# Row maxima of sparse attention scores: the mask leaves the matrix product, and one product runs on two halves of the array

## The chip, the cores and the metric

The kernel runs on one core of a Trainium2 chip. The metric is the device time of one launch in microseconds (us). The core has TensorE (PE in the profile; its weight loads are PEld), VectorE (DVE), ScalarE (ACT), GpSimd (POOL) and SyncE (SP, which here only issues DMAs).

## The reference

A block-sparse attention of 4 batches and 8 heads, 768 positions, head size 64, is followed by a mixture of 8 experts in which every token goes through every expert. The change touches only the attention.

```python
scores = scale * np.matmul(q, k.transpose(0, 1, 3, 2))       # 768 x 768 for each of 32 heads
mask = np.abs(blk_i - blk_j) <= window                       # blocks of 32 positions; one mask for all heads
mask = mask | (blk_i == 0) | (blk_j == 0) | (blk_i == n_blocks - 1) | (blk_j == n_blocks - 1)
...                                                          # and 3 sampled blocks for each block of rows
scores = np.where(mask, scores, -1000000000.0)
scores = scores - np.max(scores, axis=-1, keepdims=True)
attn = np.exp(scores)
attn = attn / (np.sum(attn, axis=-1, keepdims=True) + 1e-09)
return np.matmul(attn, v).astype(np.float32)
```

## The kernel before

**The attention.** Heads are taken one after the other (n = 0 to 31), each as NC = 6 tiles of 128 rows. A number q or k is kept as two float16 parts, high and low. For a head, a tile `qt` (and `kt`) holds two transposed layers of 128 rows: q layer 0 has the high part in rows 0 to 63 and the low part in rows 64 to 127; q layer 1 has the high part again in rows 0 to 63, then 24 rows that say which block a position lies in, and later two rows with the row maximum. k layer 0 has the high part twice, k layer 1 the low part in rows 0 to 63 and 24 rows of walls (0, or a large negative number) beside it. So layer 0 gives high·high + low·high, and layer 1 gives high·low plus the mask.

Every tile is multiplied twice. `scores(n, c)` makes S of a tile with q rows on the partitions, in a PSUM tile of two banks (`sc`, pool `ps_s`, three of them), and VectorE takes its maximum over 768 columns (L676). `lower(n)` writes the six maxima of a head back into q's layer 1 (through GpSimd and a transposing DMA), and `weights(T)` makes the transposed tile with the maximum already subtracted, so that ScalarE can take the exponential at once (L708). `split_lo` (L718, L720, L722) turns the exponential's low half into float16 on the engine that the planner holds for the least loaded; `values` multiplies with v in 18 small products for each half of a tile (L765).

**The order.** It is written out by hand. `at(T, order, function, ...)` puts a step at time T, one T for each of the 192 tiles; the steps are recorded in order of T, and each engine keeps that order. Head n starts at T0 = 6n: `scores(n, c)` stands at T0 - 10 + c, `lower(n)` at T0 - 4, `weights` at T0 + c. The two transposes `turn(n, 0)` and `turn(n, 1)`, which fill `qt` and `kt` by DMA, stand at T0 - 16 and T0 - 14; `load_qk` for every second head at T0 - 30. All these DMAs are issued by SP, one after the other, and use one queue. A planner (`WORK`, `charge`, `lightest`, with `STEP` microseconds for each T) adds up costs for VectorE, ScalarE and GpSimd; it decides only where `split_lo` goes.

**The rest.** While the last heads run, the first expert's weights are loaded (`load_w(1, 0)`, one DMA of 2 MB at T = 100) and prepared. From about 400 us on, the experts' products fill TensorE (L1213 and L1345); the change does not touch them.

Of the kernel before, what the change touches and what calls it, by code (L numbers as in the profile page):

```python
# [8 lines left out]
F16 = mybir.dt.float16  # L9
F32 = mybir.dt.float32  # L10
# [34 lines left out]
HQ = 300  # L45
NHA = 10
LATE = 34
STEP = 2.03
LLO = 1
LEADM = 10  # L50
LAV = 3


@with_exitstack
def tile_sparse_attention_moe(
# [27 lines left out]
    CH = NC // 2  # L83
    TH = S // 2
# [85 lines left out]

    wr = {}

    def load_w(which, e):
        src, n, w = (w1, KD, FF) if which == 1 else (w2, KF, DM)
        t = raw.tile([P, KD * FF], F32, tag="r", name=f"r{which}_{e}")
        t = t.rearrange("p (c f) -> p c f", f=w)
        nc.sync.dma_start(out=t, in_=src[e].rearrange("(c p) f -> p c f", p=P))
        wr[which] = t

    def scale_steps(which, e, vector=nc.vector, scalar=nc.scalar):  # L180
# [213 lines left out]
    with ExitStack() as actx:  # L394
# [16 lines left out]
        aconst = pool("aconst", 1)  # L411
# [4 lines left out]
        ROWS_M, ROWS_T = D + NB, D + 34  # L416
        AT_M = D + 32
        HALVES = ((0, 512), (512, S))

        vsp = pool("vsp", 1)  # L420
        xw = pool("xw", 2)
        col = pool("col", 8)
        ps_s = pool("ps_s", 3, space=PSUM)
# [236 lines left out]
        tops = {}  # L660

        def scores(n, c):
            qt, kt = qts[n % NSET], kts[n % NSET]
            sc = ps_s.tile([P, 1024], F32, tag="sc", name=f"m_{n}_{c}")
            ka, kb_ = (kt[:, l].rearrange("p c t -> p (c t)") for l in range(2))
            for lo, hi in HALVES:
                nc.tensor.matmul(  # L667
                    sc[:, lo:hi], lhsT=qt[:, 0, c], rhs=ka[:, lo:hi], start=True, stop=False
                )
                nc.tensor.matmul(  # L670
                    sc[:, lo:hi], lhsT=qt[:ROWS_M, 1, c], rhs=kb_[:ROWS_M, lo:hi],
                    start=False, stop=True,
                )
            if c == 0:
                tops[n] = col.tile([P, NC], F32, tag="top", name=f"top_{n}")
            nc.vector.tensor_reduce(  # L676
                out=tops[n][:, c : c + 1], in_=sc[:, :S], axis=AX.X, op=ALU.max
            )

        def lower(n):  # L680
            t = qss[n % NQS]
# [12 lines left out]
        def weights(T):  # L694
# [3 lines left out]
            qa, qb = (qt[:, l].rearrange("p c t -> p (c t)") for l in range(2))  # L698
            for lo, hi in HALVES:
                nc.tensor.matmul(  # L700
# [26 lines left out]
        def lightest():  # L727
# [3 lines left out]
            return engine  # L731

        WORK = {
            scores: (0.95, 0.0, 0.0), weights: (0.0, 0.9, 0.0),
            lower: (0.0, 0.0, 1.05),
            high_qk: (0.0, 0.93, 0.0), low_qk: (0.65, 0.0, 0.0), peak: (0.0, 1.04, 0.0),
            scale_qk: (1.3, 0.0, 0.69), scale_v: (1.0, 0.0, 0.0), peak_v: (0.94, 0.0, 0.0),
# [81 lines left out]
        NPAIR = B * NHP  # L819
        for g in range(NPAIR):  # L820
            T0 = 2 * NC * g
            at(T0 - 30, FIRST, load_qk, g)
            at(T0 - 26 if g != 1 else -14, LATER, peak, g, 0)
            at(T0 - 24 if g != 1 else -14, LATER, peak, g, 1)
            at(T0 - 20, TURNS, spread_qk, g)
            at(T0 - 20, LATER, scale_qk, g)
        for n in range(B * H):
            T0 = NC * n
            for m in range(2):
                T1 = T0 + 2 * m if n != 1 else m + 3  # L830
                at(T1 - 19, LATER, high_qk, n, m)
                at(T1 - (17 if n != 1 else 18), LATER, low_qk, n, m)
                at(T1 - 16, FIRST, turn, n, m)
            for c in range(NC):
                at(T0 - LEADM + c, SCORES, scores, n, c)
            at(T0 - LEADM + NC, TOPS, lower, n)
        for T in range(NTILE):
            at(T + LAV, VALUES, values, T, 0)
# [8 lines left out]
        for b in range(B):  # L847
            T0 = b * H * NC
# [12 lines left out]
        at(22, LATER, scale_part, "g", 0, 1, wg.rearrange("p c e -> p (c e)"))  # L861
        at(23, TURNS, scale_spread, "g")
        at(23, LATER, split_gate)
        at(-31, FIRST, lay_blocks)
        at(-21, LATER, near_fence)
        at(-20, LATER, far_fence)
        at(-16, TURNS, lay_walls)

        def start_w():
            load_w(1, 0)  # L870
# [71 lines left out]
    class Pinned:  # L942
        vector, scalar, gpsimd = (InOrder(x) for x in (nc.vector, nc.scalar, nc.gpsimd))
# [562 lines left out]
```

## Time and profile before

| | |
|---|---|
| three runs | 2205.54, 2207.67, 2208.66 us; median 2207.67 |
| the profiled execution | 2205.67 us, of which the span of the profile is 2203.8 |
| TensorE busy | 2158.5 us, 98% of the span |
| VectorE, ScalarE, GpSimd busy | 1699.3, 1288.6 and 1434.1 us |
| granted TensorE clock | 0.998 |
| attention | to about 400 us; 168 of its 192 tiles belong to heads 4 to 31 |

A row of the timeline gives the start, the duration, the engine, the line of the code, and the tile written and read. A matmul's duration runs until its result has landed, so several overlap; what one costs in a dense stream is the distance to the next one's start. In the groups by line, the last column is the engine's idle time before these instructions and what ended it.

### The profile page before, as it was taken

To read this page: it belongs to the slowest core of one execution; us is meant where nothing else is said; L and a number is where in the kernel's file an instruction comes from. 1 tells how busy PE (TensorE), PEld (TensorE's weight loads), DVE (VectorE), ACT (ScalarE), POOL (GpSimd) and SP (SyncE) were. 2 spreads that over 40 slices of the span, in tenths; PEclk is the share of its full clock that TensorE was granted. 3 is DMA by queue.
4 is the path that set the end of the run, shared out by engine and by line. 5 is a ranking of instruction groups with operands and counts; after the bars stand their busy time and mean duration, and the time that the engine had idled before them with its cause. 6 is when DMAs were issued, how large, how long until landed. Compare 5 with 4: busy or idle time off the path is not lost.

```text
span 2203.8 us, 47209 instructions
## 1 busy us (share of the span) xinstructions
PE 2158.5 (98%) x18892; PEld 1598.9 (73%) x18892; DVE 1699.3 (77%) x2927; ACT 1288.6 (58%) x2393; POOL 1434.1 (65%) x1481
## 2 busy tenths in 40 slices
PE   6999999999999999999999999999999999999999
PEld 4777777667767777777777777777777777777777
DVE  8878888786878768876887688768876887688765
ACT  5788888766466556554655465546554655465442
POOL 5556678677558656865686568656865676568553
PEclk9999999999999999999999999999999999999999
DMA  7667866322121212121212121212121212121221
GB/s 169 143 143 156 208 134 149 104 87 96 59 89 51 89 51 90 51 90 51 89 51 89 51 89 51 90 51 89 51 90 51 89 51 89 51 89 58 80 80 51
DMA packets 195345, 192.36 MB, mean 87 GB/s; under 512 B 132124, under 2 KB 150580, under 8 KB 195124
## 3 DMA queue, kind: packets, MB, share of 16 engines
q1 hardware_dynamic: 194560, 189.30, 31.3%
q8 instruction: 148, 2.42, 0.5%
q14 instruction: 73, 0.60, 0.1%
q10 hardware_dynamic: 564, 0.03, 0.0%
HBM read 140.54 MB, written 17.30 MB: 72 GB/s over the span
## 4 chain that ended last, share of the span: by engine, by line
PE 63%; DVE 6%; POOL 5%; ACT 3%; issue 2%; DMA 0%; POOLq 0%; DVEq 0%; SPq 0%
PE py L1345 32%; PE p L1213 31%; ACT h L1234 1%; POOL s L1293 1%; POOL h L1245 1%; DVE attic L1076 1%; POOL r L1087 1%; DVE h L1245 1%; DVE a L1225 1%; DVE acc L1369 1%; DVE u L1225 1%; POOL r L1094 1%; DVE arena L1076 1%; POOL c L1094 1%; POOL a L1094 1%
## 5 line engine op out<-in xcount | busy, mean ns | idle before, releaser
L1345 PE MATMUL py<-w2p,h 128*128 128x256 f16 x8064 | 974.1, 273 | 3.7 <-ACT w2p L1072 1.1
L1345 PEld LDWEIGHTS <-h 128*128 128x128 f16 x8064 | 789.5, 98 | 156.7 <-issue 5.0
L1245 POOL TENSOR_TENSOR h<-u,h 128x384 f16<-128x384 f32 x128 | 126.1, 985 | 522.0 <-ACT h L1234 522.0
L1213 PEld LDWEIGHTS <-attic 128*128 128x128 f16 x3072 | 299.7, 98 | 174.4 <-DVE attic L1076 6.7
L1213 PE MATMUL p<-attic 128*128 128x384 f16 x2304 | 421.2, 326 | 3.9 <-DVE attic L1076 2.1
L1213 PE MATMUL p<-arena 128*128 128x384 f16 x2304 | 417.4, 326 | 5.3 <-DVE arena L1076 1.8
L1369 DVE SCALAR_TENSOR_TENSOR acc<-py,spare,acc 128x256 f32<-128x256 f32 (+1 forms) x588 | 299.6, 514 | 91.1 <-PE py L1345 85.5
L1234 ACT ACTIVATE h<-c 128x384 f16<-128x384 f32 x256 | 132.5, 518 | 348.8 <-DVE c L1225 301.9
L1213 PEld LDWEIGHTS <-arena 128*128 128x128 f16 x2304 | 225.2, 98 | 129.6 <-issue 5.1
L1225 DVE SCALAR_TENSOR_TENSOR a<-p,a 128x384 f32<-128x384 f32 x384 | 211.2, 550 | 21.0 <-PE p L1213 8.6
L1245 DVE TENSOR_TENSOR h<-s,h 128x384 f16<-128x384 f32 x128 | 113.8, 889 | 145.1 <-ACT h L1234 145.0
L676 DVE TENSOR_REDUCE top<-m 128x1 f32<-128x768 f32 x192 | 181.8, 951 | 48.5 <-PE m L670 47.7
L708 ACT ACTIVATE pe<-t,qk 128x768 int32<-128x768 f32 x192 | 172.4, 900 | 70.2 <-PE t L703 62.9
L1094 POOL TENSOR_TENSOR c<-c,r 128x384 f32<-128x384 f32 x128 | 159.0, 1242 | 10.0
L1234 ACT ACTIVATE h<-r 128x384 f16<-128x384 f32 x256 | 129.8, 516 | 60.2 <-POOL r L1094 58.6
L1094 POOL TENSOR_TENSOR r<-s,r 128x384 f32<-128x384 f32 x128 | 157.6, 1231 | 10.0
L1293 POOL TENSOR_TENSOR s<-a,u 128x384 f32<-128x384 f32 x128 | 133.1, 1040 | 30.6 <-ACT a L1290 29.8
L1245 POOL TENSOR_TENSOR h<-r,h 128x384 f16<-128x384 f32 x128 | 145.3, 1135 | 5.8 <-ACT h L1234 5.8
L1213 PE MATMUL p<-arena,attic 128*128 128x384 f16 x768 | 146.1, 326 | 1.1 <-DVE a L1225 1.1
L722 POOL TENSOR_SCALAR pl<-pe 128x768 f16<-128x768 uint16 x112 | 96.7, 867 | 71.3 <-ACT pe L708 70.1
L667 PE MATMUL m<-kt,qt 128*128 128x512 f16 (+1 forms) x384 | 127.8, 333 | 9.8 <-DMA kt<-ks 6.6
L1094 POOL TENSOR_TENSOR a<-a,r 128x384 f32<-128x384 f32 x128 | 128.5, 1004 | 10.0
(207 smaller groups left out, 3677.6 us busy)
## 6 DMA issues: line engine op xcount, KB each, us to landing
arena<-xd SPq DMA_DIRECT2D x128, 384.0 KB, 3.5
attic<-xd SPq DMA_DIRECT2D x96, 384.0 KB, 3.5
r<-in_moe_w_dram SPq DMA_DIRECT2D x16, 2048.0 KB, 8.5
arena<-in_q_dram SPq DMA_DIRECT2D x16, 384.0 KB, 4.1
arena<-in_k_dram SPq DMA_DIRECT2D x16, 384.0 KB, 4.6
arena<-in_v_dram SPq DMA_DIRECT2D x4, 1536.0 KB, 7.8
xd<-xs_t SPq DMA_DIRECT2D x16, 384.0 KB, 2.7
out_dram<-acc SPq DMA_DIRECT2D x48, 128.0 KB, 1.7
```

The lines of the kernel that those rows point to most:

```text
L667: nc.tensor.matmul(sc[:, lo:hi], lhsT=qt[:, 0, c], rhs=ka[:, lo:hi], start=True, stop=False)
L676: nc.vector.tensor_reduce(out=tops[n][:, c : c + 1], in_=sc[:, :S], axis=AX.X, op=ALU.max)
L708: nc.scalar.activation(pe, sc[:, :S], AF.Exp, bias=EXP_SHIFT, scale=qk[n // 2][3])
L722: nc.gpsimd.tensor_scalar(lo, low, FINE, 1.0, ALU.mult, ALU.mult)
L1094: nc.gpsimd.tensor_tensor(out=out, in0=x, in1=y, op=ALU.subtract)
L1213: nc.tensor.matmul(ps, lhsT=w1p[p][:, l, kc, fs], rhs=xp[p][:, r, kc], start=(kc == 0 and m == 0), stop=(kc == KH - 1 and m == 2),)
L1225: nc.vector.scalar_tensor_tensor(out=t, in0=ps, scalar=HDOWN, in1=other, op0=ALU.mult, op1=ALU.add)
L1234: nc.scalar.activation(h[:, 0], src, AF.Relu if relu else AF.Copy)
L1245: eng.tensor_tensor(out=h[:, 1], in0=src, in1=h[:, 0], op=ALU.subtract)
L1293: nc.gpsimd.tensor_tensor(out=s1, in0=a1, in1=u3, op=ALU.add)
L1345: nc.tensor.matmul(py, lhsT=hs[i, p, kc][:, l, tsl], rhs=w2p[p][:, r, kc], start=(old is None and kc == 0 and m == 0), stop=(kc == KF // 2 ...
L1369: nc.vector.scalar_tensor_tensor(out=dst, in0=src, scalar=c, in1=dst, op0=ALU.mult, op1=ALU.add)
```

## The change

For heads 4 to 31 the scores for the maximum are made differently; heads 0 to 3 stay as they were (`NPLAIN = 4`).

- **The mask leaves the product.** Once, at T = 7 to 12, `wall(c)` multiplies the 24 block rows alone (two matmuls on rows 64 to 87, into a tile of `ps_s`), and ScalarE copies the result into `walled`, a bfloat16 tile in SBUF. From then on VectorE's `tensor_tensor_reduce` adds `walled` to the scores, writes the sum back into PSUM, and takes the maximum with it; it is built as two instructions, the second of which writes out the one column of maxima.
- **The third product shrinks to 64 rows.** A tile's 768 columns are cut into 384 + 384, in two banks. Layer 0 is multiplied as before, in all 128 rows, by two matmuls of 384 columns. Layer 1 needs only rows 0 to 63 now: the first half of the columns is multiplied in the array's upper 64 rows, the second half in its lower 64 rows.
- **Copies for the lower rows.** Operands for rows 64 to 127 have to lie in partitions 64 to 127. `twin(n, m)` copies them there by DMA from SP: `qx` (64 x 768) from q layer 1, at T0 - 13, and `kx` (64 x 384) from the second half of k, of which it takes layer 0, the high part, at T0 - 12.
- **The first expert's weights** come as four DMAs (T = 100, 106, 112, 118) where one was.
- The planner's `STEP` goes from 2.03 to 1.93 and its cost of `scores` on VectorE from 0.95 to 1.05, which moves `split_lo`: VectorE 39 to 23 tiles, ScalarE 41 to 38, GpSimd 112 to 131.

```diff
-STEP = 2.03
+STEP = 1.93
+WALLT = -5
...
+        walled = aconst.tile([P, NC, S], BF16, name="walled")
...
+            UP, DOWN = slice(0, D), slice(D, P)
+            side = [sc[:, b * 512 : b * 512 + TH] for b in range(2)]
...
+            qx, kx = twins[n % NSET]
+            for b in range(2):
+                nc.tensor.matmul(side[b], lhsT=qt[:, 0, c], rhs=k0[b], start=True, stop=False)
+            nc.tensor.matmul(side[0], lhsT=qt[UP, 1, c], rhs=k1[0][UP], start=False, stop=True)
+            nc.tensor.matmul(
+                side[1], lhsT=qx[DOWN, c], rhs=kx[DOWN].rearrange("p c t -> p (c t)"),
+                start=False, stop=True,
+            )
+            both = sc.rearrange("p (b s) -> p b s", b=2)[:, :, :TH]
+            nc.vector.tensor_tensor_reduce(
+                out=both, in0=both, in1=walled[:, c].rearrange("p (b s) -> p b s", b=2),
+                scale=1.0, scalar=LOWEST, op0=ALU.add, op1=ALU.max, accum_out=top,
+            )
+
+        def twin(n, m):
+            x = (qts, kts)[m][n % NSET]
+            nc.sync.dma_start(
+                out=twins[n % NSET][m][D:],
+                in_=(x[:D, 0, CH:] if m else x[:D, 1]),
+            )
+
+        def wall(c):
...
+            if n >= NPLAIN:
+                at(T0 - 13, FIRST, twin, n, 0)
+                at(T0 - 12, FIRST, twin, n, 1)
...
+        for c in range(NC):
+            at((NPLAIN - 2) * NC + WALLT + c, SCORES, wall, c)
```

**TensorE, one tile of scores between two halves of `values`** (`m` is the scores' PSUM tile, `qt`, `kt` the transposed tiles, `pl` and `pe` the exponential's parts, `u` the product with v). Before:

```order
L667 LDWEIGHTS qt_101
L667 MATMUL m_2_2753<-kt_105,qt_101 128x512
L670 LDWEIGHTS qt_101
L670 MATMUL m_2_2753<-kt_105,qt_101 128x512
L667 LDWEIGHTS qt_101
L667 MATMUL m_2_2753<-kt_105,qt_101 128x256
L670 LDWEIGHTS qt_101
L670 MATMUL m_2_2753<-kt_105,qt_101 128x256
L765 LDWEIGHTS pl_1_2653
```

Now, at the same place (L705 is the product in rows 0 to 63, L706 the one in rows 64 to 127):

```order
L704 LDWEIGHTS qt_101
L704 MATMUL m_2_2804<-kt_105,qt_101 128x384
L704 LDWEIGHTS qt_101
L704 MATMUL m_2_2804<-kt_105,qt_101 128x384
L705 LDWEIGHTS qt_101
L705 MATMUL m_2_2804<-kt_105,qt_101 128x384
L706 LDWEIGHTS qx_128
L706 MATMUL m_2_2804<-kx_129,qx_128 128x384
L820 LDWEIGHTS pl_1_2704
```

The number of instructions is the same; 512 + 512 + 256 + 256 columns have become four times 384, the last two in half of the rows each.

**SP, the DMAs of one head of an even number**: its two transposes, between them the maxima of the head two before it, then the loads for a later pair. Before:

```order
L655 DMA_TRANSPOSE qt_102<-qs_109 128x12x128
L688 DMA_TRANSPOSE qt_104<-qs_110 128x6x128
L655 DMA_TRANSPOSE kt_106<-ks_113 128x12x128
L591 DMA arena<-in_q_dram 128x2x384
L591 DMA arena<-in_k_dram 128x2x384
L655 DMA_TRANSPOSE qt_103<-qs_110 128x12x128
```

Now:

```order
L671 DMA_TRANSPOSE qt_102<-qs_111 128x12x128
L743 DMA_TRANSPOSE qt_104<-qs_109 128x6x128
L671 DMA_TRANSPOSE kt_106<-ks_113 128x12x128
L718 DMA qx_130<-qt_102 64x768
L607 DMA arena<-in_q_dram 128x2x384
L607 DMA arena<-in_k_dram 128x2x384
L718 DMA kx_131<-kt_106 64x384
L301 DMA xd_76<-xs_t_3820 128x1536
L671 DMA_TRANSPOSE qt_103<-qs_109 128x12x128
```

Two copies have come in, one ahead of the loads of q and k and one behind them; each waits for its transpose to land, and SP's later DMAs stand behind it.

More of the change, by code (lines that the diff above doesn't have):

```diff
@@ L171, in tile_sparse_attention_moe, with load_w @@
     wr = {}
-    def load_w(which, e):
+    def load_w(which, e, pieces=1):
         src, n, w = (w1, KD, FF) if which == 1 else (w2, KF, DM)
@@ L176, in load_w, with piece @@
         t = t.rearrange("p (c f) -> p c f", f=w)
-        nc.sync.dma_start(out=t, in_=src[e].rearrange("(c p) f -> p c f", p=P))
+        x = src[e].rearrange("(c p) f -> p c f", p=P)
         wr[which] = t
+        m = n // pieces
+        def piece(j):
+            nc.sync.dma_start(out=t[:, j * m : (j + 1) * m], in_=x[:, j * m : (j + 1) * m])
+        piece(0)
+        return piece
     def scale_steps(which, e, vector=nc.vector, scalar=nc.scalar):
@@ L418, in tile_sparse_attention_moe @@
         HALVES = ((0, 512), (512, S))
+        NPLAIN, LOWEST = 4, -3.0e38
+        twins = [
+            tuple(
+                sets.tile([P, w, P], F16, name=f"{nm}_{i}") for nm, w in (("qx", NC), ("kx", CH))
+            )
+            for i in range(NSET)
+        ]
+        walled = aconst.tile([P, NC, S], BF16, name="walled")
         vsp = pool("vsp", 1)
@@ L664, in scores @@
             sc = ps_s.tile([P, 1024], F32, tag="sc", name=f"m_{n}_{c}")
-            ka, kb_ = (kt[:, l].rearrange("p c t -> p (c t)") for l in range(2))
+            if c == 0:
+                tops[n] = col.tile([P, NC], F32, tag="top", name=f"top_{n}")
+            top = tops[n][:, c : c + 1]
+            if n < NPLAIN:
+                ka, kb_ = (kt[:, l].rearrange("p c t -> p (c t)") for l in range(2))
+                for lo, hi in HALVES:
+                    nc.tensor.matmul(
+                        sc[:, lo:hi], lhsT=qt[:, 0, c], rhs=ka[:, lo:hi], start=True, stop=False
+                    )
+                    nc.tensor.matmul(
+                        sc[:, lo:hi], lhsT=qt[:ROWS_M, 1, c], rhs=kb_[:ROWS_M, lo:hi],
+                        start=False, stop=True,
+                    )
+                nc.vector.tensor_reduce(out=top, in_=sc[:, :S], axis=AX.X, op=ALU.max)
+                return
@@ new lines, in scores @@
+            UP, DOWN = slice(0, D), slice(D, P)
+            side = [sc[:, b * 512 : b * 512 + TH] for b in range(2)]
+            k0, k1 = (
+                [kt[:, l, b * CH : (b + 1) * CH].rearrange("p c t -> p (c t)") for b in range(2)]
+                for l in range(2)
+            )
+            qx, kx = twins[n % NSET]
+            for b in range(2):
+                nc.tensor.matmul(side[b], lhsT=qt[:, 0, c], rhs=k0[b], start=True, stop=False)
+            nc.tensor.matmul(side[0], lhsT=qt[UP, 1, c], rhs=k1[0][UP], start=False, stop=True)
@@ L666, in scores @@
+        def wall(c):
+            n = NPLAIN - 1
+            qt, kt = qts[n % NSET], kts[n % NSET]
+            E = slice(D, D + NB)
+            sc = ps_s.tile([P, 1024], F32, tag="sc", name=f"wall_{c}")
             for lo, hi in HALVES:
                 nc.tensor.matmul(
-                    sc[:, lo:hi], lhsT=qt[:, 0, c], rhs=ka[:, lo:hi], start=True, stop=False
-                )
[L670 to L678, printed above, removed]
+                    sc[:, lo:hi], lhsT=qt[E, 1, c],
+                    rhs=kt[:, 1].rearrange("p c t -> p (c t)")[E, lo:hi], start=True, stop=True,
+                )
+            nc.scalar.activation(walled[:, c], sc[:, :S], AF.Copy)
         def lower(n):
@@ L733, in tile_sparse_attention_moe @@
         WORK = {
-            scores: (0.95, 0.0, 0.0), weights: (0.0, 0.9, 0.0),
+            scores: (1.05, 0.0, 0.0), wall: (0.0, 0.9, 0.0), weights: (0.0, 0.9, 0.0),
             lower: (0.0, 0.0, 1.05),
@@ L821, in tile_sparse_attention_moe @@
             T0 = 2 * NC * g
[L822 to L826, printed above, removed]
+            back = 0
+            at(T0 - 30 - back, FIRST, load_qk, g)
+            at(T0 - 26 - back if g != 1 else -14, LATER, peak, g, 0)
+            at(T0 - 24 - back if g != 1 else -14, LATER, peak, g, 1)
+            at(T0 - 20 - back, TURNS, spread_qk, g)
+            at(T0 - 20 - back, LATER, scale_qk, g)
         for n in range(B * H):
@@ L869, in start_w @@
         def start_w():
-            load_w(1, 0)
+            piece = load_w(1, 0, KD)
+            for j in range(1, KD):
+                at(100 + 6 * j, FIRST, piece, j)
             parts, whole, spread, power = scale_steps(1, 0)
@@ L1488 @@
     from concourse.bass_utils import run_bass_kernel_spmd as _run
-    nc = _bacc.Bacc("TRN2", target_bir_lowering=False, num_devices=1)
+    nc = _bacc.Bacc("TRN2", target_bir_lowering=False, num_devices=1, dynamic_dma_scratch_size=4096)
     arrays, args = {}, []
```

5 lines of the change are left out of this document (added).

## The prediction

> **What bounds the kernel now.** I read the page's head first, for the engine that is never idle:
>
> ```profile
> span 2203.8 us, 47209 instructions
> PE 2158.5 (98%) x18892; PEld 1598.9 (73%) x18892; DVE 1699.3 (77%) x2927; ACT 1288.6 (58%) x2393; POOL 1434.1 (65%) x1481
> ```
>
> A busy TensorE says little by itself, since overlapping matmuls count as busy. So next came the table of stretches, cut along the attention (columns: length, then PE, PEld, DVE, ACT, POOL busy):
>
> ```profile
> 30.00:50.00 20.00, 19.33 (x207) 12.32 (x206) 16.48 (x25) 12.61 (x16) 13.59 (x21) 0.86 0.72 133
> 50.00:150.00 100.00, 99.97 (x1374) 72.34 (x1373) 80.01 (x134) 77.49 (x105) 53.86 (x89) 1.00 0.65 134
> 150.00:300.00 150.00, 148.28 (x2112) 107.69 (x2108) 127.37 (x202) 126.83 (x182) 96.96 (x146) 1.00 0.77 174
> 300.00:400.00 100.00, 95.73 (x1346) 69.25 (x1344) 87.25 (x132) 81.98 (x108) 82.98 (x97) 1.00 0.65 143
> ```
>
> TensorE is idle 0.03 us of 100, then 1.7 of 150, and only at the end 4.3 of 100. Third, the groups by line and shape between 60 and 400 us, for what ends the idle time of the other engines:
>
> ```profile
> L676 DVE TENSOR_REDUCE top<-m 128x1 f32<-128x768 f32 x167 | 158.4, 951 | 41.4 <-PE m L670 40.6
> L708 ACT ACTIVATE pe<-t,qk 128x768 int32<-128x768 f32 x167 | 150.0, 900 | 58.5 <-PE t L703 52.1 <-DVE xn L786 1.3 <-POOL pl L722 1.2
> L722 POOL TENSOR_SCALAR pl<-pe 128x768 f16<-128x768 uint16 x98 | 84.2, 863 | 61.9 <-ACT pe L708 60.9
> L718 DVE TENSOR_SCALAR pl<-pe 128x768 f16<-128x768 uint16 x28 | 21.7, 773 | 0.0
> ```
>
> 167 tiles in 340 us make a step of 2.036 us. VectorE waits for TensorE's scores, 41.4 / 167 = 0.25 us a step; ScalarE waits for TensorE's weights; GpSimd waits for ScalarE. Nobody of weight is waited for by TensorE: the attention runs at its rate. Last the timeline of TensorE, to see that it is dense in starts and not only in overlaps:
>
> ```profile
> 199.66 0.38 PE L667 MATMUL m<-kt,qt 128*128 128x512 f16 x1
> 199.87 0.38 PE L670 MATMUL m<-kt,qt 88*128 88x512 f16 x1
> 200.09 0.27 PE L667 MATMUL m<-kt,qt 128*128 128x256 f16 x1
> 200.21 0.27 PE L670 MATMUL m<-kt,qt 88*128 88x256 f16 x1
> 200.32 0.19 PE L765 MATMUL u<-vq,pl 128*128 128x66 f16 x1
> ...
> 200.59 0.38 PE L700 MATMUL t<-qt,kt 128*128 128x512 f16 x1
> ...
> 201.52 0.38 PE L667 MATMUL m<-kt,qt 128*128 128x512 f16 x1
> ```
>
> From one tile of scores to the next 1.86 us, of which the scores take 200.32 - 199.66 = 0.66. The rest up to 2.036 is transposes, logits and little idleness.
>
> **The products of a tile.** A 384-column matmul shows its price later in the kernel, in the chain of waits (start, length, what):
>
> ```profile
> 565.17 2.94 PE p L1213 x18
> ```
>
> 0.163 us each. The two on layer 0 make 0.33. The two of 64 rows are 0.163 if they run side by side, 0.33 if one after the other; the nearest row on how soon a second weight load and matmul can follow is the one on the walls' layout below (six matmuls in one piece), 0.025 apart, so side by side I take 0.163 + 0.025 = 0.19. Without any cost of changing between the full array and its halves the tile would fall from 0.66 to 0.52.
>
> That cost is the unknown of this change: twice in each tile the array goes from 128-row to 64-row operation and back. The trace has one place where a full-array matmul is followed by one of fewer rows, at the start:
>
> ```profile
> 4.71 0.69 DVE L472 TENSOR_SCALAR plan<-attic 24x768 bf16<-24x768 f32 x1
> ...
> 6.71 0.47 PE L615 MATMUL u<-ident,qk 128*128 128x128 f32 x1 [0.73 <-ACT unread L108]
> 7.11 0.10 PEld L524 LDWEIGHTS <-plan 24*128 24x128 bf16 x1 [0.22 <-DVE attic L503]
> ...
> 9.29 0.31 PE L524 MATMUL u<-fence,plan 24*128 24x24 bf16 x6 [2.11 <-DVE fence L519]
> ...
> 18.71 0.64 PE L615 MATMUL u<-ident,qk 128*128 128x128 f32 x2
> 18.92 0.15 PEld L667 LDWEIGHTS <-qt 128*128 128x128 f16 x1
> ```
>
> The weights of L524 lie in `plan`, ready at 5.40, yet they are loaded at 7.11, 0.40 us after the matmul in front of them started. Behind the same kind of matmul at 18.71 (two, 0.21 apart) the full-array load starts at 18.92, together with the second of them. So the 24-row load waited for the matmul to run out: 0.40 - 0.21 = 0.19 us past the end of its stream. DVE L503 is named as the releaser, but it writes a tile that the load does not read. In that stretch matmuls were spaced twice as far as later (the same pair of L615 starts inside 0.25 us at 203.39):
>
> ```profile
> 203.39 0.41 PE L615 MATMUL u<-ident,qk 128*128 128x128 f32 x2
> 203.63 0.38 PE L667 MATMUL m<-kt,qt 128*128 128x512 f16 x1
> ```
>
> At twice the rate, 0.19 becomes 0.097. With 0.025 from weight load to matmul, a change costs 0.12 into the halves. Out of them fewer rows have to run out; I take 0.09, an estimate without a row of its own. Bounds for the two together: nothing, if the one row has another cause, and 2 x 0.215 = 0.43, if the wait does not shrink with the rate. I take 0.21, because the only row that shows such a change is nearer to it than to either end. A tile then takes 0.33 + 0.19 + 0.21 = 0.73, that is 0.07 more than before; break-even is at 0.14. Over the 168 tiles of heads 4 to 31: **+11.8 us**.
>
> The Trainium skill's page TensorEngine Tiling (Array Packing), section Tiling Modes, says that changing the tiling mode, unlike changing the tile, drains TensorE; the row at 7.11 agrees, and the page gives no time for it. The page TensorE: Matmul & The Clock Gate, Part 3, lets matmuls on different row tiles start about 4 ns apart; by that figure the pair would be 0.167, an estimate, and the tile term 0.05 x 168 = 8 us; no run here shows it yet.
>
> **Walls.** Six steps at T = 7 to 12, each with 512 + 256 columns (0.22 + 0.11 from the distances above) in 24 rows and its own two changes, 0.21: 6 x 0.54 = **+3.2 us**, between 2 and 4.6. ScalarE's six copies (0.90 each, as L708) are hidden: in 30 to 50 us ScalarE is busy 12.6 of 20, and these steps are longer; uncovered they would add 2 us.
>
> **VectorE.** The new operation reads PSUM and SBUF, writes PSUM, and has a second instruction for the column of maxima. Rows that bound it: the plain maximum above at 0.951 and the slowest kind of two-operand operation on 768 columns; for the second instruction, small ones.
>
> ```profile
> L581 DVE SCALAR_TENSOR_TENSOR vl<-arena,sv,vh 128x768 f16<-128x768 f32 x8 | 10.6, 1321 | 0.0
> L784 DVE TENSOR_SCALAR r<-u 128x6 f32<-128x6 f32 x28 | 4.5, 162 | 6.0 <-PE u L765 5.9
> L108 ACT ACTIVATION_READ_ACCUMULATOR unread<-arena 128x1 f32 x24 | 4.6, 194 | 0.0
> L1225 DVE SCALAR_TENSOR_TENSOR a<-p,a 128x384 f32<-128x384 f32 x384 | 211.2, 550 | 21.0 <-PE p L1213 8.6
> ```
>
> L1225, which takes one operand from PSUM and one from SBUF like the new one, does 384 columns in 0.55; at the plain maximum's rate that is what 384 columns and a fixed start would cost, so I take 0.95 + 0.16 = 1.11 (bounds 0.95 and 1.52). That is +0.16 a tile, and 16 `split_lo` of 0.773 leave VectorE: 168 x 0.16 - 12 = 15 us over the attention, 0.08 a step, against 0.25 of waiting for TensorE. Cost on the path: nothing, while TensorE's step does not shrink. VectorE's step is 1.71 by the stretches (80.0 + 127.4 + 87.3 busy in 350 us, times 2.036). If TensorE got faster by 0.14, VectorE's 1.71 + 0.08 would fill 1.79 of 1.90, and part of the gain would go into its queue. GpSimd gets 19 splits more, 16 us; it has 61.9 us of waiting for ScalarE.
>
> **Copies.** SP issues two more DMAs for each of 28 heads; `kx` must land before the fourth matmul of the head's first tile. One even head, from SP's timeline and TensorE's, and the landing times:
>
> ```profile
> 204.53 1.30 SPq L655 DMA_TRANSPOSE kt<-ks  x1
> 205.88 1.03 SPq L591 DMA_DIRECT2D arena<-in_q_dram  x1
> 206.96 0.47 SPq L591 DMA_DIRECT2D arena<-in_k_dram  x1
> ...
> 211.58 0.38 PE L667 MATMUL m<-kt,qt 128*128 128x512 f16 x1
> ```
>
> ```profile
> DMA to landing us min/median/max: 3.6/3.8/8.8
> out_dram<-acc SPq DMA_DIRECT2D x48, 128.0 KB, 1.7
> arena<-in_k_dram SPq DMA_DIRECT2D x12, 384.0 KB, 4.6
> ```
>
> The transpose (first row of the three) lands at 204.53 + 3.8 = 208.3; a copy of 48 KB, with the 1.7 of the smallest row, at about 210.3: 1.3 us in time. In even heads the loads of q and k stand ahead of it on the queue and land at 206.96 + 4.6 = 211.6, about when it is needed. Late by 0 to 1 us in 14 heads: 0 to 14 us; I take **+1**, since the fourth matmul comes half a microsecond after the tile's start. What stands behind the waiting copies on SP is the next head's transpose, issued at 212, which has room. The four pieces of the first expert's weights move 2 MB as before: nothing.
>
> **Sum.** 11.8 + 3.2 + 1, less 2 because TensorE idles 4.3 us in 300 to 400 and part of a longer step fits there: +14. On the profiled execution's 2205.7 that is **2220**; this execution lies 2.0 below the median of the runs shown, so against 2207.7 it is +12. Everything behind the attention starts as much later.
>
> **Rivals.**
> - *Faster: the change between full and half array is cheap* (0 to 0.07 a tile for both). For it: the row at 7.11 is single, behind a transposing float32 matmul and at half rate. TensorE gives 0.14 to 0.07 a tile, 24 to 12 us; VectorE's queue takes some of the larger gain, walls and copies 3 to 5: -6 to -18, 2188 to 2200. The decision falls at 0.14 us for both changes; below it the kernel gains.
> - *The halves run one after the other, or the wait does not shrink with the rate*: +0.14 or +0.22 a tile more, 24 to 37 us: 2243 to 2257. Against it: nothing in the rows, except that the operands and the PSUM banks of the two are disjoint.
> - *VectorE becomes the bound*: at 1.52 a tile its step is 1.71 + 0.57 - 0.07 = 2.21 against 2.11: about 0.1 x 168 + 14, 2236. Against it: L1225 shows no such price with an operand in PSUM.
> - *Nothing comes of it*: changes of 0.10 to 0.17 together cancel what the shorter product saves, 2203 to 2211.
>
> **Chances.** The forecast 0.41 (2212 to 2230), cheap changes 0.39, serial halves 0.05, VectorE 0.06, cancelled 0.09. This kernel's measurement tells 0.2%, 4.4 us, from no change. Slower: 0.39 of the forecast's 0.41 and the two dear rivals, 0.50; the same: 0.09 + 0.02 = 0.11; faster: 0.39. Signs being split, the range takes both: 2188 to 2240, which leaves out some 0.07 above and 0.07 below.
>
> **What would show it.** Right: in the new timeline some 0.1 us or more between the end of the second 384-column stream and the start of the half-array pair, and again before the next L765; a scores block near 0.73 and a step near 2.1 us; VectorE still waiting for TensorE. The cheap rival: both gaps under 0.04 and a step near 1.9. Serial halves: starts of the pair 0.16 apart. Late copies: TensorE's waits name the DMA of `kx`. VectorE as bound: TensorE waits for the scores' PSUM tile. What would make the prediction wrong is, above all, that the one row it prices the change from does not speak for 64 rows in a warm stream.

## The result, and the profile after

The changed kernel takes 2225.69 us (median of 4 runs, 2223.56 to 2227.22), the kernel before on the same chip 2207.14: 18.5 us more, a ratio of 1.0083 with a 95% interval from 1.0066 to 1.0101. The profiled execution has a span of 2224.9 us. The prediction said 2220 (2188 to 2240), with a chance of 0.50 for "slower" and 0.39 for "faster".

The page's head of the changed kernel:

```profile
span 2224.9 us, 47647 instructions
PE 2168.8 (97%) x18904; PEld 1567.1 (70%) x18904; DVE 1695.7 (76%) x3079; ACT 1290.8 (58%) x2396; POOL 1438.8 (65%) x1500
```

TensorE has 21 us of span more and 10 us of busy time more, so half of the loss is new idleness. The stretches show where it lies (length; then PE, PEld, DVE, ACT, POOL busy; granted TensorE clock, busy share of the DMA engines, GB/s):

```profile
30.00:50.00 20.00, 18.56 (x206) 11.50 (x206) 17.01 (x25) 14.41 (x18) 14.05 (x21) 1.00 0.80 143
50.00:150.00 100.00, 99.18 (x1313) 60.69 (x1310) 77.66 (x174) 73.31 (x98) 53.15 (x88) 1.00 0.65 140
150.00:300.00 150.00, 142.65 (x1938) 87.58 (x1936) 112.78 (x242) 116.99 (x169) 94.18 (x140) 0.99 0.81 178
300.00:400.00 100.00, 94.71 (x1319) 58.80 (x1320) 85.23 (x179) 80.04 (x107) 76.89 (x102) 1.00 0.62 138
```

Read the second and third rows against those of before: TensorE was idle 0.03 us of 100 and 1.7 of 150, now 0.8 and 7.4; it started 1374 and 2112 matmuls in the same stretches, now 1313 and 1938. VectorE, with a dearer operation on paper, is less busy. From the start of head 4's first exponential to the start of the attention's last one it is 353.8 us instead of 335.6; what follows is as long as before (1789.4 and 1789.3). All that is left of the loss stands ahead of head 4: that first exponential starts at 81.6 us instead of 78.9. The two profiled executions differ in clock too, as their rows of 30 to 50 us show (0.86 and 1.00): within the attention it was granted at 0.5 from 28.8 to 35.6 us before, and from 249.1 to 252.5 now.

One tile of scores, from TensorE's timeline, and the weight loads in the same tile:

```profile
201.27 0.49 PE L704 MATMUL m<-kt,qt 128*128 128x384 f16 x2
201.69 0.33 PE L705 MATMUL m<-kt,qt 64*128 64x384 f16 x1
201.70 0.33 PE L706 MATMUL m<-kx,qx 64*128 64x384 f16 x1
201.96 0.20 PE L820 MATMUL u<-vq,pl 128*128 128x66 f16 x1
```

```profile
201.69 0.09 PEld L705 LDWEIGHTS <-qt 64*128 64x128 f16 x1 [0.32 <-issue]
201.69 0.09 PEld L706 LDWEIGHTS <-qx 64*128 64x128 f16 x1
201.96 0.10 PEld L820 LDWEIGHTS <-pl 128*128 128x128 f16 x1 [0.17 <-ACT pe L763]
```

Two 384-column streams are over 0.325 after the first start, at 201.60; the half-array weights are loaded only at 201.69. The pair starts together and would be through at 201.86, and the next full-array weights come at 201.96. Over the tiles of the attention the medians of the distances between starts are 0.258 from the last full-array start to the pair (0.095 beyond its stream of 0.163), 0.003 within the pair, and 0.265 from there to the next matmul (0.102 beyond). So the two changes take 0.197 us a tile, and the whole block of scores 0.690; before it was 0.659. That is why the halves do not pay even by themselves: running the third product in two halves saves one stream, 0.163, and the two changes cost 0.197. But 0.031 in 168 tiles is 5.2 us; most of the 18.5 us lies elsewhere.

VectorE's new operation and its readout, by line and shape between 60 and 420 us, and the same in its timeline:

```profile
L711 DVE CUSTOM_DVE_ANT_0 m<-m,walled 128x768 f32<-128x768 f32 x168 | 161.5, 962 | 62.2 <-PE m L706 24.1 <-ACT pe L763 22.5 <-ACT unread L109 6.7
...
L705 PEld LDWEIGHTS <-qt 64*128 64x128 f16 x167 | 15.5, 93 | 53.3 <-issue 53.3
...
L711 DVE DVE_READ_ACCUMULATOR2_ANT top<- 128x1 f32 x168 | 23.6, 141 | 0.0
```

```profile
244.79 0.97 DVE L711 CUSTOM_DVE_ANT_0 m<-m,walled 128x768 f32<-128x768 f32 x1 [0.27 <-PE m L706]
245.68 0.14 DVE L711 DVE_READ_ACCUMULATOR2_ANT top<- 128x1 f32 x1
245.68 0.62 DVE L665 SCALAR_TENSOR_TENSOR qs<-arena,qk,qs 128x384 f16<-128x384 f32 x1
```

The readout starts 0.89 after the operation, and the next operation starts with it. Adding the mask has cost VectorE next to nothing over the plain maximum's 0.951. The row of L705 is the change into the halves seen as idle time of the weight loads: 53.3 / 167 = 0.32 us a tile in which no weights are loaded ahead.

Last, TensorE's longest waits between 50 and 420 us (what waited, for what; us in total, times, longest):

```profile
PE m L706 <- DMA kx<-kt: 6.2, 8, 1.7
PE u L820 <- POOL pl L777: 2.5, 4, 0.7
PE t L758 <- DMA qt<-qs: 2.1, 2, 1.2
PE t L755 <- DVE top L711: 1.4, 4, 0.5
```

In 8 heads the lower half's product waits for the copy of k, which is the largest wait there is. The longest of these waits, 1.72 us, begins at 246.6 us, and the stretch at half clock, from 249.1 to 252.5, follows close behind it. If matmuls run half as fast there, it costs half of its 3.4 us, 1.7, as much again as the wait itself; this is an estimate.

### The profile page after: what moved, and what is told of

Read it like the earlier page. It is cut to its first block, busy times and chain, and to the rows that moved or that the text cites. A ratio compares the mean times of both kernels' runs of the same rounds, so it can differ in the third digit from the quotient of the medians.

```text
span 2224.9 us, 47647 instructions
## 1 busy us (share of the span) xinstructions
PE 2168.8 (97%) x18904; PEld 1567.1 (70%) x18904; DVE 1695.7 (76%) x3079; ACT 1290.8 (58%) x2396; POOL 1438.8 (65%) x1500
## 4 chain that ended last, share of the span: by engine, by line
PE 59%; DVE 7%; POOL 6%; ACT 4%; issue 3%; DMA 1%; POOLq 0%; DVEq 0%; SPq 0%; ACTq 0%
PE py L1408 30%; PE p L1276 29%; ACT h L1297 1%; POOL h L1308 1%; POOL s L1356 1%; DVE h L1308 1%; POOL r L1150 1%; DVE attic L1139 1%; DVE a L1288 1%; DVE acc L1432 1%; DVE u L1288 1%; DVE h L1302 1%; POOL r L1157 1%; DMA r<-in_moe_w_dram 1%; POOL c L1157 1%
## 5 line engine op out<-in xcount | busy, mean ns | idle before, releaser
L711 DVE CUSTOM_DVE_ANT_0 m<-m,walled 128x768 f32<-128x768 f32 x168 | 161.5, 962 | 62.2 <-PE m L706 24.1
L777 POOL TENSOR_SCALAR pl<-pe 128x768 f16<-128x768 uint16 x131 | 112.2, 861 | 74.2 <-ACT pe L763 72.7
L820 PEld LDWEIGHTS <-pl 128*128 128x128 f16 x1152 | 106.0, 97 | 47.7 <-issue 21.3
```

The source lines that it names most:

```text
L711: nc.vector.tensor_tensor_reduce(out=both, in0=both, in1=walled[:, c].rearrange("p (b s) -> p b s", b=2), scale=1.0, scalar=LOWEST, op0=AL ...
L777: nc.gpsimd.tensor_scalar(lo, low, FINE, 1.0, ALU.mult, ALU.mult)
L820: nc.tensor.matmul(uv[:, c], lhsT=l[:, c * P : (c + 1) * P], rhs=w[:, h, kc, :], start=(kc == 0 and c == 0 and m == 0), stop=(kc == NC - 1 ...
```

## The experiments

Times are medians; each ratio is to the kernel before on the same chip, whose medians lay between 2207.14 and 2207.31. The rows come from several chips, and a ratio is an estimate of its own, not exactly the quotient of the medians.

| kernel | us | ratio, 95% interval |
|---|---|---|
| after | 2225.69 | 1.0083 [1.0066, 1.0101] |
| no_kx | 2220.64 | 1.0062 [1.0049, 1.0074] |
| no_copies | 2218.52 | 1.0048 [1.0034, 1.0062] |
| full_rows | 2215.05 | 1.0033 [1.0021, 1.0044] |
| full_one_w | 2210.08 | 1.0016 [1.0006, 1.0025] |
| vector_mask | 2211.80 | 1.0023 [1.0015, 1.0032] |
| planner | 2207.15 | 1.0000 [0.9992, 1.0009] |
| pairs | 2218.68 | 1.0052 [1.0040, 1.0065] |
| serial | 2236.71 | 1.0139 [1.0125, 1.0153] |
| four_changes | 2268.55 | 1.0282 [1.0268, 1.0297] |
| no_third | 2196.46 | 0.9947 [0.9932, 0.9962] |
| plain_max | 2179.88 | 0.9879 [0.9866, 0.9893] |
| plain_step | 2186.37 | 0.9910 [0.9896, 0.9924] |

**full_rows**: the third product in the full array's 88 rows, no copies; the walls, VectorE's sum with the mask, the planner's numbers and the four weight DMAs stay.

```diff
-            nc.tensor.matmul(side[0], lhsT=qt[UP, 1, c], rhs=k1[0][UP], start=False, stop=True)
-            nc.tensor.matmul(side[1], lhsT=qx[DOWN, c], ...)
+            for b in range(2):
+                nc.tensor.matmul(
+                    side[b], lhsT=qt[:ROWS_M, 1, c], rhs=k1[b][:ROWS_M], start=False, stop=True
+                )
...
-            if n >= NPLAIN:
-                at(T0 - 13, FIRST, twin, n, 0)
-                at(T0 - 12, FIRST, twin, n, 1)
```

> As the changed kernel, but layer 1 is multiplied in the full array again (two matmuls of 384 columns in 88 rows, so the mask is added once by the product and once by VectorE); no copies, no change between full and half array. Walls, VectorE's new operation, the planner's numbers and the four weight DMAs stay. Theory (the changes of rows cost about 0.20 us a tile, against 0.163 saved, and the late copies of k cost 7.6 us): 2225.7 - 7 - 7.6 = 2211, between 2208 and 2214. Rival (VectorE's operation, which holds the scores' PSUM tile longer, or the planner's numbers carry most of the loss): 2218 or more.

2215.05: between the two, just above the expected range. The halves and their copies are more than half of the loss, but 7.9 us remain that have nothing to do with them.

**no_kx**: layer 0 of `kt` holds the high part of k in rows 0 to 63 and again in 64 to 127, so the lower half can read it where it stands.

```diff
-                side[1], lhsT=qx[DOWN, c], rhs=kx[DOWN].rearrange("p c t -> p (c t)"),
+                side[1], lhsT=qx[DOWN, c], rhs=k0[1][DOWN],
...
-                at(T0 - 12, FIRST, twin, n, 1)
```

> As the changed kernel, but the lower rows read k straight from rows 64 to 127 of kt's layer 0, which hold the same numbers as kx; the copy of k is gone, the copy of q stays. Theory (the matmul in the lower rows waits 7.6 us in all for kx): 2218, between 2216 and 2220, and no wait of that matmul for a DMA in the trace. Rival (the copy of q, or SP's queue as a whole, is as late): 2223 or more, with the wait now named after qx or after the transposes.

2220.64, just above the range, and no wait for `kx` is left: 5.1 us by the medians for a copy of 48 KB a head, though the intervals overlap (1.0066 to 1.0074). In this run's profile, its slowest execution, TensorE waits 4.3 us for transposes of q instead of 2.1, so the rival may hold in part. Why `kx` came late, from SP's timeline in `after` (start, length, what), with TensorE's fourth matmul of that head in the second fence:

```profile
238.28 1.42 SPq L671 DMA_TRANSPOSE kt<-ks  x1
239.75 1.73 SPq L183 DMA_DIRECT2D r<-in_moe_w_dram  x1
241.53 0.47 SPq L718 DMA_DIRECT2D qx<-qt  x1
242.05 0.58 SPq L607 DMA_DIRECT2D arena<-in_q_dram  x1
242.68 0.49 SPq L607 DMA_DIRECT2D arena<-in_k_dram  x1
243.41 0.47 SPq L718 DMA_DIRECT2D kx<-kt  x1
```

```profile
246.25 0.33 PE L705 MATMUL m<-kt,qt 64*128 64x384 f16 x1
248.30 0.32 PE L706 MATMUL m<-kx,qx 64*128 64x384 f16 x1 [1.72 <-DMA kx<-kt]
```

Here a piece of the expert's weights, the copy of q and the loads of q and k stand ahead of `kx`; it is issued at 243.4 and the matmul that needs it can start only 4.9 us later. Over the kernel the median from issue to landing of `kx` is 3.1 us.

**no_copies**: on top of it, the lower half's weights are rows 64 to 127 of q's layer 0, which hold q's low part where `qx` held the high part.

```diff
-                side[1], lhsT=qx[DOWN, c], rhs=k0[1][DOWN],
+                side[1], lhsT=qt[DOWN, 0, c], rhs=k0[1][DOWN],
...
-                at(T0 - 13, FIRST, twin, n, 0)
```

> As the changed kernel, but neither copy is made: the lower rows multiply rows 64 to 127 of qt's and kt's layer 0 (so q's low part stands where q's high part stood). SP's queue is as before the change. Theory: nothing more to gain beside the copy of k, 2217, between 2215 and 2220. Rival (issuing the copies delays the transposes that TensorE's weights stage waits for): 2 to 5 us below the run without kx.

2218.52, another 2.1 us, which the intervals of these two do not tell apart; both copies together, 7.2 us, they do.

**pairs**: on no_copies, two tiles share one change into the halves and one out of them (four full products, then four half products).

```diff
+            if n >= NPLAIN and c % 2:
+                return
...
+            for i in range(2):
+                for b in range(2):
+                    nc.tensor.matmul(sides[i][b], lhsT=qt[:, 0, c + i], rhs=k0[b], ...)
+            for i in range(2):
+                nc.tensor.matmul(sides[i][0], lhsT=qt[UP, 1, c + i], rhs=k1[0][UP], ...)
+                nc.tensor.matmul(sides[i][1], lhsT=qt[DOWN, 0, c + i], rhs=k0[1][DOWN], ...)
```

> As the run without copies, but two tiles share one change into the half array and one out of it: four full matmuls, then four half ones, then VectorE's two maxima. Theory (each change costs 0.1 us whatever follows it): 0.20 us less for each pair of tiles, 84 x 0.20 = 17 us below the run without copies, 2200, between 2197 and 2205, and so below the kernel before. Rival (two score tiles at once take two of the three PSUM tiles, and TensorE waits for VectorE): 2212 or more.

2218.68: nothing gained. The changes are indeed halved, as the weight loads' idle time ahead of the halves shows (first fence): 26.9 us in 84 places, where no_copies has 53.3 in 168. But two tiles now reach VectorE at once. It waits up to 3.2 us for the next scores (second fence; 1.6 in no_copies), and what stands in its queue behind two maxima comes late for TensorE: `xn` and `top` are waited for where they were not, or less (third fence, TensorE's longest waits).

```profile
PEld L711 <- issue: 26.9, 84, 0.6
```

```profile
DVE m L719 <- PE m L714: 57.6, 67, 3.2
```

```profile
PE u L860 <- DVE xn L850: 3.4, 12, 0.7
PE u L631 <- DVE xn L850: 2.8, 11, 0.7
PE t L767 <- DMA qt<-qs: 2.7, 2, 2.0
PE t L764 <- DVE top L719: 2.6, 3, 2.0
```

All of TensorE's waits of this list make 19.9 us, in no_copies 9.6, which covers 10 of the missing 17 us. Two waits of 2.0 us are each followed by 3.4 us at a granted clock of 0.5, which no_copies does not have: by the estimate above 3.4 us more. The rest has no row. The rival had the time right but not the reason: hardly any wait stands ahead of a scores matmul (0.4 us), as it would if their PSUM tiles were short. My expectation costed the changes alone and left out the order in which VectorE gets its work.

**serial** and **four_changes**: on no_copies, the two half products one after the other in the upper rows; and full, half, full, half, that is four changes a tile in place of two.

```diff
-                side[1], lhsT=qt[DOWN, 0, c], rhs=k0[1][DOWN],
+                side[1], lhsT=qt[UP, 1, c], rhs=k1[1][UP],
```

```diff
-            for b in range(2):
-                nc.tensor.matmul(side[b], lhsT=qt[:, 0, c], rhs=k0[b], start=True, stop=False)
+            nc.tensor.matmul(side[0], lhsT=qt[:, 0, c], rhs=k0[0], start=True, stop=False)
             nc.tensor.matmul(side[0], lhsT=qt[UP, 1, c], rhs=k1[0][UP], start=False, stop=True)
+            nc.tensor.matmul(side[1], lhsT=qt[:, 0, c], rhs=k0[1], start=True, stop=False)
```

> The run without copies (2218.5), with both products of 64 rows in rows 0 to 63, one after the other (q high by k low for both halves of the columns). The number of changes of rows stays two a tile; only the overlap is gone. Theory (the pair now starts 3 ns apart, so the overlap is worth a whole stream of 0.163): 168 x 0.16 = 27 us more, 2245, between 2240 and 2250, with the second start 0.163 behind the first. Rival (the overlap of starts in the trace is not one of work): under 2230.

> The run without copies, in another order: full product of the first half, its product of 64 rows, full product of the second half, its product of 64 rows. Four changes of rows a tile for two, and no overlap. Theory (0.095 into the half array, 0.105 out of it): against the serial run another 0.20 a tile, 168 x 0.20 = 34 us, so 2279, between 2270 and 2288. Rival (a change costs only once, or is hidden behind the longer block): 2250 or less.

One tile of four_changes in TensorE's timeline:

```profile
201.07 0.32 PE L703 MATMUL m<-kt,qt 128*128 128x384 f16 x1
201.33 0.33 PE L704 MATMUL m<-kt,qt 64*128 64x384 f16 x1
201.59 0.34 PE L705 MATMUL m<-kt,qt 128*128 128x384 f16 x1
201.86 0.33 PE L706 MATMUL m<-kt,qt 64*128 64x384 f16 x1
202.13 0.20 PE L820 MATMUL u<-vq,pl 128*128 128x66 f16 x1
```

Every step is 0.26 to 0.27: a stream of 0.163 and a change of 0.10. The median block is 0.690 in no_copies, 0.849 in serial and 1.058 here, so the price of a change is confirmed by two kernels that differ in little else. The times rose by 18.2 and by another 31.8 us, where the blocks, times 168 tiles, say 26.7 and 35.1. I had expected nearly all of it. Part of the rest went into idle time that was there anyway: in the stretches of serial TensorE is as busy in the first row as in no_copies (99.95), and busier in the second (no_copies: 95.29):

```profile
50.00:150.00 100.00, 99.95 (x1237) 57.92 (x1235) 73.48 (x164) 68.94 (x93) 50.00 (x83) 1.00 0.61 125
...
300.00:400.00 100.00, 98.17 (x1255) 57.52 (x1254) 83.10 (x176) 76.20 (x104) 71.73 (x97) 1.00 0.62 129
```

**planner**: the kernel before with `STEP = 1.93` and `scores` at 1.05, nothing else.

```diff
-STEP = 2.03
+STEP = 1.93
...
-            scores: (0.95, 0.0, 0.0), weights: (0.0, 0.9, 0.0),
+            scores: (1.05, 0.0, 0.0), weights: (0.0, 0.9, 0.0),
```

> The kernel before with two numbers of the change alone: STEP 1.93 for 2.03 and 1.05 for the cost of scores on VectorE, so that split_lo goes to the engines almost as in the changed kernel. The run in full rows, without any change of rows, lost 7.9 us; its walls account for 2.7 of them by the trace. Theory (most of the other 5 is splits that now land late for the products with v): 2209 to 2212. Rival (the planner's numbers do nothing; VectorE's operation or the four weight DMAs cost the 5): 2206 to 2208.

2207.15, as the rival said: the planner's numbers cost this kernel nothing. They do move the splits; by line and shape in 60 to 400 us, GpSimd now has 115 of them where it had 98:

```profile
L722 POOL TENSOR_SCALAR pl<-pe 128x768 f16<-128x768 uint16 x115 | 97.9, 856 | 53.5 <-ACT pe L708 51.5 <-DMA xd<-xs_b 0.9
```

**vector_mask** and **full_one_w**: full_rows with the weights in one DMA, the first with the planner's old numbers as well.

```diff
-            piece = load_w(1, 0, KD)
-            for j in range(1, KD):
-                at(100 + 6 * j, FIRST, piece, j)
+            load_w(1, 0)
```

> The run in full rows with the planner's numbers and the single weight DMA of the kernel before: what is left of the change is the walls, VectorE's addition and maximum, and the cut into 384 + 384 columns. Theory (walls 2.7 us, VectorE's operation nothing, since its rows show 0.96 us and a readout that overlaps): 2210, between 2208 and 2212. Rival (VectorE's operation costs the rest): 2213 to 2216, as the run in full rows.

> The run in full rows with the first expert's weights in one DMA again; the planner's numbers stay as in the changed kernel. It stands between the run in full rows (2215.1) and the one with the mask on VectorE alone (2211.8), which differ in the planner's numbers and in the weight DMAs. Theory (the four pieces, each ahead of transposes on the queue, cost those 3 us): 2211 to 2213. Rival (the planner's numbers, harmless in the kernel before, cost them here): 2214 to 2216.

2211.80 and 2210.08, not told apart from each other; the second lies just below its range. Against full_rows, the single DMA saves 5.0 us by the medians; the two intervals still touch (1.0021 to 1.0025), and by the ratios it is 3.8. In the traces TensorE waits for late transposes of q, full_rows in the first fence, full_one_w in the second.

```profile
PE t L757 <- DMA qt<-qs: 3.5, 3, 1.4
```

```profile
PE t L757 <- DMA qt<-qs: 1.2, 2, 1.1
```

That is 2.3 us more, but not all of it can come from the pieces: of full_rows' three waits the first, 1.03 us, ends at 176.3, long before the first piece is issued at 235.0, and the last, at 416.7, has its like in full_one_w at 413.3. Only 1.41 us, ending at 276.6, stands among the pieces. The profile of full_rows has besides two stretches of 3.4 us at a granted clock of 0.5 (from 178.6 and 509.7 us) that full_one_w has not. Clock alone is not the answer either: executions with a mean clock of 0.998 are 2214.0 and 2212.84 us in full_rows and 2210.1 in the median in full_one_w, 3.3 apart. So the four pieces cost some 3 to 5 us, and through what is not shown.

**no_third**: `after` without the third product, in halves or otherwise, and without copies.

```diff
-                nc.tensor.matmul(side[b], lhsT=qt[:, 0, c], rhs=k0[b], start=True, stop=False)
-            nc.tensor.matmul(side[0], lhsT=qt[UP, 1, c], rhs=k1[0][UP], start=False, stop=True)
-            nc.tensor.matmul(side[1], lhsT=qx[DOWN, c], ...)
+                nc.tensor.matmul(side[b], lhsT=qt[:, 0, c], rhs=k0[b], start=True, stop=True)
```

> As the changed kernel, but the third product (q high by k low, 64 rows) is left out of the scores for the maximum altogether, with its copies; the maximum serves as a shift of the exponent, which the sum of the exponentials takes out again. No changes of rows, and 0.33 us less on TensorE than in the kernel before. If TensorE alone set the step: 2207 + 2.7 - 168 x 0.33 = 2154. Theory (VectorE, at 1.8 us a step, and ScalarE take over as the bound): between 2165 and 2185. Rival (waits for VectorE between tiles eat nearly all): 2195 or more.

2196.46. TensorE's blocks lost 0.36 us (0.690 less two streams), 60 us over 168 tiles; the time fell by 22 against no_copies, as the rival said. The others cannot keep up: TensorE waits for VectorE's maxima, the transposes and GpSimd's split, in its longest waits between 50 and 400 us, and the granted clock there is 0.5 for 13.7 us in three stretches, which no_copies has not:

```profile
PE t L750 <- DVE top L706: 10.0, 15, 1.2
PE t L753 <- DMA qt<-qs: 7.2, 4, 2.7
PE u L815 <- POOL pl L772: 7.2, 12, 1.4
```

**plain_max** and **plain_step**: the kernel before with layer 0 alone under the maximum, in all heads, without mask; the second with `STEP = 1.9` and `scores` at 1.05 besides.

```diff
-                    sc[:, lo:hi], lhsT=qt[:, 0, c], rhs=ka[:, lo:hi], start=True, stop=False
-                )
-                nc.tensor.matmul(
-                    sc[:, lo:hi], lhsT=qt[:ROWS_M, 1, c], rhs=kb_[:ROWS_M, lo:hi],
-                    start=False, stop=True,
+                    sc[:, lo:hi], lhsT=qt[:, 0, c], rhs=ka[:, lo:hi], start=True, stop=True
                 )
```

> The kernel before with one product less: the scores for the maximum are made of layer 0 alone, without mask and without the third product, for all heads; so the shift is the maximum over all columns, masked ones too. No walls, no copies, VectorE's plain maximum. TensorE loses 0.33 us a tile, 63 us in 192 tiles. Theory (VectorE's 1.71 us and ScalarE's step become the bound, as in the run without the third product, less the 2.7 us of walls): between 2158 and 2182, the fastest of all. Rival (as for that run): 2195 or more.

> The fastest run so far (layer 0 alone for the maximum, no mask, 2179.9), with the planner told 1.05 for VectorE's maximum and 1.9 us a step: 19 splits on VectorE for 39, 135 on GpSimd for 112. In that run VectorE was busy 297 of 330 us and TensorE waited for it. Theory (VectorE is the bound, 20 splits of 0.77 less): 5 to 15 us less, 2165 to 2175. Rival (GpSimd's later splits keep the products with v waiting instead): 2178 or more.

plain_max is the fastest of all, 27 us below the kernel before. The maximum only shifts the exponent, so it need not be that of the exact, masked scores; how far below it the largest allowed score of a row may lie depends on the data, and other data were not tried. TensorE waits most for VectorE (first fence, its two longest waits between 50 and 380 us). Moving splits from VectorE to GpSimd, as plain_step does, halves that wait and makes a new one (second fence), and the time is 6.5 us worse, as the rival said.

```profile
PE t L696 <- DVE top L672: 17.5, 29, 1.7
PE t L699 <- DMA qt<-qs: 4.7, 4, 2.1
```

```profile
PE u L761 <- POOL pl L718: 10.6, 15, 2.5
PE t L696 <- DVE top L672: 9.6, 18, 1.0
```

## Why the prediction was right, and where it was not

The kernels from before to after make a ladder; its first rung holds several edits, the others one each:

| edit | runs | us |
|---|---|---|
| mask on VectorE, walls, 384 + 384, planner | full_one_w less before | 2.9 |
| weights in four DMAs | full_rows less full_one_w | 5.0 |
| third product in halves | no_copies less full_rows | 3.5 |
| copy of q | no_kx less no_copies | 2.1 |
| copy of k | after less no_kx | 5.1 |

By the ratios the rungs are 3.5, 3.8, 3.3, 3.1 and 4.6 us: one rung is known to 1 or 2 us. The intervals at both ends of the 3.5, the 2.1 and the 5.1 overlap, those of the 5.0 touch; what stands clear is the first rung and both copies together, 7.2. Each rung is measured in the presence of those above it in the table: a weight piece that makes `kx` later counts with `kx` here.

- **The cost of changing the array: right.** The prediction took 0.21 a tile for both changes, from one row at 7.11 us; measured 0.197. The rival "cheap changes" needed 0.07 or less, and "does not shrink with the rate" 0.43; both are out by the block's medians and by four_changes. That the load at 7.11 waits for the matmul, and not for the write of DVE L503 that the profile names, is borne out: in all 14 profiles it comes 0.40 to 0.41 us behind that matmul's start, and in serial, where the matmul is earlier, 0.07 us before that write is over. The way out, 0.102, had no row in the prediction; that 0.09 came near it is luck. The Trainium skill's page TensorEngine Tiling (Array Packing), section Tiling Modes, says that such a change drains TensorE; the weights that are loaded only 0.09 after the stream's end agree.
- **The tile term, +11.8: too large.** The pair starts 0.003 apart, not 0.025, and so does the first matmul behind its weights. The block is 0.690 and not 0.73: 0.031 x 168 = 5.2 us, or 6.2 against the 0.653 of full_rows, of which 3.5 reach the time. The 4 ns that the Trainium skill states for matmuls on different row tiles (TensorE: Matmul & The Clock Gate, Part 3) was the better figure here; the prediction gave the term by it as 8 us.
- **The halves run side by side: right.** serial shows the other case, 0.173 apart and 18 us more.
- **The copies, +1: mis-sized, 7.2.** The step that failed is the landing time: 1.7 us, from the smallest transfer of another kind, where 3.1 was the median of `kx`, and 4.9 us went by from its issue to the matmul in the head above. What the queue held ahead of it was named; that a weight piece would stand there too was not.
- **The weight pieces, "nothing": too low, some 3 to 5.** The prediction counted bytes. Where a piece stands on SP's queue can matter: in the head above one is issued ahead of `kx`. But in full_rows and full_one_w, which make no copies, the traces do not show how the pieces cost the time, and that stays open.
- **VectorE, nothing: right.** 1.11 was taken, 0.962 measured, and the readout is hidden beside the next operation.
- **Walls, +3.2: near.** Head 4's first exponential comes 2.7 us later in `after`, whose profile lacks the stretch at half clock near 30 us. In full_one_w, which has it as before has (29.6 to 36.4), it comes at 82.7, 3.8 later. That includes whatever else moved ahead of it; no run left out the walls alone.
- **The planner's numbers, nothing: right** (2207.15). **Two us absorbed by late stalls: right in kind**; serial swallowed 8.5 of 26.7.

So the mechanism of the tile term was right, but that the forecast came within 6 us is luck, since its errors partly cancelled: the tile term, with what it was said to absorb, 11.8 - 2 where 3.5 was measured, 6 too high; copies and weight pieces 1 where 12.2 was measured by the medians, 11 too low. The forecast's sign did rest on the part that was argued, 0.197 against the 0.163 saved; of the measured loss two thirds are copies and weight pieces, which it put at next to nothing. The chance of 0.39 for a gain was too high for a reason the prediction did not use: no_third, in which the third product costs nothing at all, gained only 10.9 us without copies, so that halves with free changes could hardly have gained much beside 7.2 us of copies.

## What to carry to other kernels

A product split into two half-array matmuls amid full-array work pays only if the stream it saves is longer than the two changes: here 0.163 against 0.197, so streams of 384 columns lose. A small copy on a queue with other DMAs is to be priced by the landing of its neighbours there, and before a load is cut in pieces it is worth looking at what each piece is put in front of. Before batching work for one engine, look at what its consumer has queued behind the batch: pairs halved the changes and gained nothing.

## What the runs showed of the hardware that was not expected

- The pair of half-array matmuls starts 0.003 us apart, with both weight loads in the same hundredth of a microsecond.
- A change between full and half array costs 0.095 us in and 0.102 out at a granted clock of 1.00; the way out, with half the rows to run empty, is no cheaper.
- Between 60 and 600 us, 8 of the 14 profiles have stretches of 3.4 us (two of them 6.8) at a granted clock of 0.5: after at 249.1, full_rows at 178.6 and 509.7, pairs at 277.6 and 332.2. Each begins within 4 us of the start of an idle time of TensorE of 0.7 to 2.7 us; most idle times of this length are followed by none. That the idle time brings it about is not shown.
- VectorE's sum and maximum with one operand in PSUM, one in SBUF and the result in PSUM takes 0.962 us for 768 columns, where the maximum alone takes 0.951, and its readout of 0.141 runs beside the next operation.
